# Attention and mixer on one core: a second staging buffer, ten step durations by the trace, and other warm-up products

## The chip, the core and the metric

The kernel runs on one core of a Trainium2 chip. A core has a matrix engine (TensorE, in the profile PE, with its weight loads as PEld), a vector engine (VectorE, DVE), an activation engine (ScalarE, ACT), a general engine (GpSimd, POOL), and DMA queues, here issued from SyncE (SP). The metric is the device time of one execution in microseconds. The kernel before takes 1115.07 us, the median of three runs from 1113.44 to 1115.68.

## The reference

Attention over 8 batches of 8 heads, 576 positions and a head width of 64, with a mask by blocks of 64 positions. Its output, heads side by side, is the input of a mixer: a token mixing of rank 32, and two matrices with a ReLU between them.

```python
scores = scale * np.matmul(q, k.transpose(0, 1, 3, 2))
scores = np.where(block_i >= block_j, scores, -1000000000.0)
scores = scores - np.max(scores, axis=-1, keepdims=True)
attn = np.exp(scores)
attn = attn / (np.sum(attn, axis=-1, keepdims=True) + 1e-09)
x = np.matmul(attn, v).transpose(0, 2, 1, 3).reshape(8, 576, 512)

h = x.transpose(0, 2, 1) @ U @ V            # U 576 x 32, V 32 x 576
u = x + h.transpose(0, 2, 1)
out = u + np.maximum(u @ w_ch1, 0.0) @ w_ch2    # 512 x 2048, 2048 x 512
```

All is float32, and the kernel keeps that precision by splitting values in two: a rounded part and the rest.

## The kernel before, in words

**Attention.** The 64 heads go one after the other (the loop over `h`). `split_qk` loads the transposed q and k of a head (64 x 1152), copies each to a rounded form (casts to `qa` and `kk`, L1161 on ACT or L1162 on DVE) and subtracts that from the loaded values to get the rest (`qb` and `kk`, L1168 on POOL or DVE). A DMA then puts copies of `qa` and `kk` into further partitions. `maxima` makes scores (L1256, L1254 for the first product of a head) and their row maxima (L1263), turned by L1275 (ACT) or L1276 (DVE); `probabilities` makes the scores again (L1300, L1301), their exponentials (L1322), a cast (L1325) and its rest (L1330); `apply_v` multiplies by v (L1354 to L1356) and divides (reciprocal L1364). After every second head `mix` applies U and V (L1384 to L1427; L1404 and L1406 are two of its ACT casts, L1405 a subtraction on POOL, L1413 and L1416 its last products) and stores u in DRAM.

**The mixer's two parts.** The hidden 2048 units are split. The first 768 go through `ffn_chunk` in 16 chunks of 288 tokens, two per batch: load u, scale it (L600 POOL), round it (L605 ACT, `uh`), take the rest (L606 POOL, `ul`), 72 products with w1 (L617, with L622 and L625 for the ReLU and its split) and 72 with w2 (L641). Chunks 14 and 15 belong to the last batch. Their products stand at a low priority (1e6 and up) and are what PE does between the heads' products. The other 1280 units are done by `block_products` (L906) after all attention has ended: 3360 products of 288 columns, in a scheme that multiplies sums of blocks.

**Staging of the block part's weights.** `blocks_of(n)` prepares the weights for that part while the heads run, w1 for n = 0 (from the priority of head 25) and w2 for n = 1 (from that of head 45). In six passes for n = 0 and five for n = 1 it takes a staging buffer `sg`, writes seven blocks into it, each as a rounded part (L730, ACT) and a rest (L731, POOL or DVE), makes four sums of blocks on the way (L735, POOL or DVE), and stores the whole buffer to DRAM (`w_d`, L750, on SP's queue). There is one such buffer, so a pass can write only when the store of the pass before has landed. The block part loads from `w_d` later.

**What sets the order.** All work is given as steps to `Plan.add`, each with an engine, a duration in ns, a priority, what it reads and writes, and for some steps other engines with their own durations (`others`). `Plan.issue` then runs a simulation with these numbers when the program is built, and writes each engine's instructions in the order that comes out. On each engine it takes the ready step of the smallest priority number. A step that may go to several engines is left aside on one when another would finish it sooner: `max(now, until) + duration + late` there against `now + ns + late` here, where `late` is a fixed handicap of a way. `after` is the time from a step's end until its result may be used, for DMAs the flight time (`DL` = 3000 ns). Steps on POOL and those on DVE marked shared (`port`) are not run at the same time, and such a DVE step holds POOL for 200 ns more. Durations are varied by up to 2% by a fixed rule on the step's number. Until 260 us of simulated time (`WARM`) PE gets a pair of products of zeros (L1495) whenever it has nothing ready. Steps of a head have priorities of 1000 per head: those of `split_qk` 900 ahead of their head. On the chip, each engine goes through its list in that order, and waits by semaphores for what the instruction needs.

**Start.** Before the steps stand some products of zeros (L1043), nine of 128 x 128 in float32, on a memset tile `zero` (L1032).

## Time and profile before

| | before |
|---|---|
| runs (3) | 1115.07 us median, 1113.44 to 1115.68 |
| profiled execution, its own time | 1114.15 us |
| its span | 1112.4 us |
| PE busy | 1078.8 us (97%), 10484 products |
| DVE busy | 988.1 us (89%) |
| ACT busy | 695.6 us (63%) |
| POOL busy | 382.8 us (34%) |
| first and last head's reciprocal (L1364) | 22.7 and 639.0 us |
| last mixing ends | 646.7 us |
| the run of block products (L906) on the chain of waits | 699.06 us to 1109.2 us |

The page has the busy time and the number of instructions of each engine, then the span in 40 slices, the DMA queues, the chain of work that ended last (followed back from the last instruction to what released each step), and groups of instructions by line with their mean duration and the idle time ahead of them. PE's busy time holds overlapping instructions and modelled ends, so a busy PE isn't PE at its peak. The views of the trace used below are the chain in order of time, the instructions of one line or tile, the stretches (busy time and, in brackets, the number of instructions of each engine between two times, then granted clock, DMA share and GB/s), and the listing by time, whose rows read: start, duration, engine, line, operation, what it writes and reads, and in square brackets what ended the idle time before it.

### The profile page before, as it was taken

The page shows a single profiled execution, that of the slowest core. Times are in us where ns is not written, and L with a number is a line of the kernel's source. Part 1 is how long each engine was busy: PE and PEld are TensorE (multiplying, and loading weights), DVE is VectorE, ACT ScalarE, POOL GpSimd, SP SyncE. Part 2 cuts the span into 40 slices and gives each one's busy share as a digit, 9 for nine tenths or more (in the row PEclk, how much of TensorE's full clock was granted, in tenths as well). Part 3 has the DMA queues.
Part 4 walks back from the last instruction along what each step waited for, and adds up shares of the span by engine and source line. Part 5 has one row for each costly group of instructions (what it writes and reads, how often), then busy time and mean ns, then how long its engine had stood idle before and what let it go on. Part 6 is the DMA issues. An engine that isn't in the chain of part 4 may idle for free.

```text
span 1112.4 us, 27442 instructions
## 1 busy us (share of the span) xinstructions
PE 1078.8 (97%) x10484; PEld 898.6 (81%) x10484; DVE 988.1 (89%) x2045; ACT 695.6 (63%) x1422; POOL 382.8 (34%) x494
## 2 busy tenths in 40 slices
PE   9899899999999899999999999999999999999998
PEld 8788788888888777888887777777777777777776
DVE  8899899999999889999998634798989999898987
ACT  5559876777786878768877622455555545454553
POOL 4426544657546768456387621000000000000000
PEclk9999999999999999999999999999999999999999
DMA  8763556466555565665544376312314040403111
GB/s 193 176 190 106 137 156 175 124 161 167 154 166 142 148 189 168 179 169 152 144 133 144 115 229 249 107 55 75 93 37 129 1 128 1 129 21 108 39 49 43
DMA packets 91651, 141.36 MB, mean 127 GB/s; under 512 B 14784, under 2 KB 65920, under 8 KB 91520
## 3 DMA queue, kind: packets, MB, share of 16 engines
q1 hardware_dynamic: 91520, 139.61, 43.6%
q8 instruction: 82, 1.34, 0.5%
q14 instruction: 49, 0.40, 0.1%
HBM read 83.05 MB, written 37.49 MB: 108 GB/s over the span
## 4 chain that ended last, share of the span: by engine, by line
PE 59%; DVE 22%; ACT 6%; DMA 5%; POOL 4%; issue 3%; SPq 0%; POOLq 0%; DVEq 0%; ACTq 0%
PE bb L906 37%; PE bf L641 5%; DVE pp L1330 4%; PE bf L617 4%; DVE mx L1263 4%; DMA w_d<-sg 2%; DVE hl L625 1%; PE bg L641 1%; DVE kk L1168 1%; DMA raw<-in_qk_dram 1%; ACT pp L1325 1%; PE ba L1300 1%; DVE x L1369 1%; PE ba L1256 1%; POOL wr L735 1%
## 5 line engine op out<-in xcount | busy, mean ns | idle before, releaser
L906 PEld LDWEIGHTS <-wb 128*128 128x128 f16 x3360 | 328.8, 98 | 82.8
L906 PE MATMUL bb<-hh,wb 128*128 128x288 f16 x2240 | 370.4, 286 | 0.0
L906 PE MATMUL bb<-hl,wb 128*128 128x288 f16 x1120 | 237.8, 286 | 0.0
L641 PE MATMUL bf<-hh,w2h 128*128 128x288 f16 x342 | 98.6, 288 | 0.6 <-DVE hl L625 0.5
L835 ACT CAST hh<-hb 128x576 f16<-128x576 f32 (+1 forms) x96 | 56.7, 591 | 66.6 <-PE bb L906 65.3
L641 PE MATMUL bf<-hl,w2h 128*128 128x288 f16 x342 | 97.8, 286 | 0.0
L641 PE MATMUL bf<-hh,w2l 128*128 128x288 f16 x342 | 97.8, 286 | 0.0
L641 PEld LDWEIGHTS <-w2h 128*128 128x128 f16 x768 | 75.3, 98 | 20.9 <-issue 1.5
L861 DVE TENSOR_TENSOR wr<-bb,wr 128x576 f32<-128x576 f32 (+1 forms) x120 | 77.8, 654 | 15.9 <-PE bb L906 15.9
L617 PEld LDWEIGHTS <-w1h 128*128 128x128 f16 x768 | 71.9, 98 | 22.2 <-issue 4.5
L1354 PE MATMUL ba<-vv,pp 128*128 128x65 f16 x840 | 87.7, 193 | 1.1 <-DVE pp L1330 0.9
L1356 PE MATMUL ba<-vv,pp 128*128 128x65 f16 x840 | 86.9, 191 | 1.4 <-DVE pp L1330 1.4
L1355 PE MATMUL ba<-vv,pp 128*128 128x64 f16 x840 | 87.4, 195 | 0.0
L1263 DVE TENSOR_REDUCE mx<-ba 128x1 f32<-128x192 f32 (+1 forms) x190 | 86.3, 479 | 0.8 <-PE ba L1256 0.6
L1168 POOL TENSOR_TENSOR qb<-raw,qa 64x576 fp32r<-64x576 f32 x44 | 62.5, 1421 | 56.9 <-ACT qa L1161 24.7
L1354 PEld LDWEIGHTS <-pp 128*128 128x128 f16 x840 | 77.4, 96 | 3.3 <-ACT pp L1325 0.7
L1355 PEld LDWEIGHTS <-pp 128*128 128x128 f16 x840 | 77.9, 97 | 2.5 <-issue 1.4
L1356 PEld LDWEIGHTS <-pp 128*128 128x128 f16 x840 | 78.0, 99 | 1.8 <-DVE pp L1330 1.6
L1330 DVE TENSOR_TENSOR pp<-ba,pp 128x448 f16<-128x448 f32 (+1 forms) x110 | 69.4, 644 | 2.7 <-ACT pp L1325 2.5
L617 PE MATMUL bf<-uh,w1l 128*128 128x288 f16 x368 | 69.2, 287 | 0.0
L835 ACT CAST hh<-wr 128x576 f16<-128x576 f32 (+1 forms) x72 | 42.6, 592 | 39.9 <-PE bb L906 39.9
L1300 PE MATMUL ba<-qa,kk 128*128 128x192 f32 (+1 forms) x187 | 64.9, 354 | 0.8 <-ACT ut L1427 0.5
(226 smaller groups left out, 2850.2 us busy)
## 6 DMA issues: line engine op xcount, KB each, us to landing
raw<-in_qk_dram SPq DMA_DIRECT2D x63, 288.0 KB
qb<-qa SPq DMA_DIRECT2D x64, 144.0 KB
kk<-kk SPq DMA_DIRECT2D x64, 144.0 KB
o_d<-ot SPq DMA_DIRECT2D x64, 144.0 KB
wr<-o_d SPq DMA_DIRECT2D x32, 288.0 KB
vr<-in_v_dram SPq DMA_DIRECT2D x28, 320.0 KB
wb<-w_d SPq DMA_DIRECT2D x14, 640.0 KB
out_dram<-wr SPq DMA_DIRECT2D x31, 288.0 KB
```

The costliest lines, as they stand in the source:

```text
L617: nc.tensor.matmul(ps[:, :T], w()[wn][:, k, fs], m[k].ap, start=(i == 0), stop=(i == len(ops) - 1))
L641: nc.tensor.matmul(ps[:, :T], w()[wn][:, f, ms], hs[f][x].ap, start=(i == 0), stop=(i == len(ops) - 1))
L835: add("ACT", _act(size(x), True), E, lambda: nc.scalar.copy(h(), x[0]()), [x[1]], [hb])
L861: add("DVE", _dve(size(out)), E, lambda: getattr(nc.vector, op)(out[0](), x[0](), y[0]()), [x[1], y[1]], [out[1]])
L906: nc.tensor.matmul(bank[:, i, :T], w(x, k), p.ap[:, k, :], start=first and n == 0, stop=last and n == len(ops) - 1)
L1168: sub = lambda e, dst=dst, x=x, y=y: lambda: e.tensor_sub(dst, raw[:, x], f32(y))
L1263: lambda i=i, view=view: nc.vector.tensor_reduce(out=mx[:, 96 + i : 97 + i], in_=view(), op=ALU.max, axis=AX.XY if i == 4 else AX.X, negat ...
L1300: nc.tensor.matmul(o, kk[:, 0, ks], qa[:, 64 + q0 : 64 + q1], start=True, stop=False)
L1330: lambda at=at, view=view, shaped=shaped: nc.vector.tensor_sub(shaped(pl[:, at]), view(), shaped(ph[:, at])),
L1354: nc.tensor.matmul(bank[:, o : o + D + 1], ph[:, w], vv[:, y, 0 : D + 1], start=(j == 0), stop=False)
L1355: nc.tensor.matmul(bank[:, o : o + D], ph[:, w], vv[:, y, D + 1 : 2 * D + 1], start=False, stop=False)
L1356: nc.tensor.matmul(bank[:, o : o + D + 1], pl[:, w], vv[:, y, 0 : D + 1], start=False, stop=(j == i))
```

## The change

Four things. (1) `stage_r` has two staging buffers in place of one. (2) Numbers that `Plan` works with: the flight time of the store of `w_d` goes from 3000 to 6500 ns; ten kinds of ACT steps get durations longer by 20 to 130 ns; L731 and L735 on POOL go from 60 to 130 ns of fixed time; and two DVE ways do: that of the casts L1162 from 64 to 130 ns, that of the splits L1168 from 68 to 250 ns. With 1.042 x 576 that last way counts 850 ns, and 600 of lateness stand on top, against 1340 on POOL. (3) At the start four of the float32 products of zeros stay. (4) Behind them come 32 float16 products of zeros with 256 columns, in alternating rows: eight pairs that use rows 0 to 63 for the one bank and 64 to 127 for the other, then eight pairs with rows 0 to 95 and 96 to 127. What is computed of the outputs is the same. From L1046 on, lines of the changed kernel are five higher.

```diff
@@ -412 +412 @@
-        add("ACT", _act(n, True), prio, lambda: nc.scalar.activation(f32(z), f32(upp), AF.Abs), [st], [zt])
+        add("ACT", _act(n, True) + 110, prio, lambda: nc.scalar.activation(f32(z), f32(upp), AF.Abs), [st], [zt])
@@ -605 +605 @@
-                add("ACT", _act(T, True), E, lambda us=us, h=uh: nc.scalar.copy(h.ap, us.ap), [us], [uh])
+                add("ACT", _act(T, True) + 30, E, lambda us=us, h=uh: nc.scalar.copy(h.ap, us.ap), [us], [uh])
@@ -622 +622 @@
-            add("ACT", _act(T), E, lambda ps=ps, th=th: nc.scalar.activation(th.ap, ps[:, :T], AF.Relu), [ps], [th])
+            add("ACT", _act(T) + 35, E, lambda ps=ps, th=th: nc.scalar.activation(th.ap, ps[:, :T], AF.Relu), [ps], [th])
@@ -666 +666 @@
-    stage_r = ring(ap, 1, [P, 7, 2, 2, P], F16, "sg")
+    stage_r = ring(ap, 2, [P, 7, 2, 2, P], F16, "sg")
@@ -730 +730 @@
-                add("ACT", _act(m, True), pr, lambda: nc.scalar.copy(hi, src), [b[1]], [sg.parts[k]])
+                add("ACT", _act(m, True) + 60, pr, lambda: nc.scalar.copy(hi, src), [b[1]], [sg.parts[k]])
@@ -732 +732 @@
-                add("POOL", 60 + 1.98 * m, pr, sub(nc.gpsimd), [b[1]], [sg.parts[k]], others=[("DVE", _dve(m), sub(nc.vector), True, 400)])
+                add("POOL", 130 + 1.98 * m, pr, sub(nc.gpsimd), [b[1]], [sg.parts[k]], others=[("DVE", _dve(m), sub(nc.vector), True, 400)])
@@ -736 +736 @@
-                add("POOL", 60 + 1.98 * m, pr, f(nc.gpsimd), [x[1], y[1]], [out[1]], others=[("DVE", _dve(m), f(nc.vector), True, 400)])
+                add("POOL", 130 + 1.98 * m, pr, f(nc.gpsimd), [x[1], y[1]], [out[1]], others=[("DVE", _dve(m), f(nc.vector), True, 400)])
@@ -751 +751 @@
-                [parts_d[n][q]], after=DL,
+                [parts_d[n][q]], after=6500,
@@ -973 +973 @@
-                            "ACT", _act(m * T, True), E, lambda a=at_x: nc.scalar.activation(a(), a(), AF.Relu), [x], [x]
+                            "ACT", _act(m * T, True) + 130, E, lambda a=at_x: nc.scalar.activation(a(), a(), AF.Relu), [x], [x]
@@ -1042 +1042 @@
-    for _ in range(9):
+    for _ in range(4):
@@ -1043,0 +1044,5 @@
+    halves = zero.ap.bitcast(F16)
+    for x in (64, 96):
+        for _ in range(8):
+            for bank, r in ((0, slice(0, x)), (1, slice(x, P))):
+                nc.tensor.matmul(banks_f[bank][:, 0 : 2 * P], halves[r, 0:P], halves[r], start=True, stop=True)
@@ -1162 +1167 @@
-                others=[("DVE", 64 + 0.55 * S, lambda dst=dst, x=x: nc.vector.tensor_copy(dst, raw[:, x]), True, 200)],
+                others=[("DVE", 130 + 0.55 * S, lambda dst=dst, x=x: nc.vector.tensor_copy(dst, raw[:, x]), True, 200)],
@@ -1170 +1175 @@
-                "POOL", 1340, pr, sub(nc.gpsimd), [raw, a], [b], others=[("DVE", 68 + 1.042 * S, sub(nc.vector), True, 600)],
+                "POOL", 1340, pr, sub(nc.gpsimd), [raw, a], [b], others=[("DVE", 250 + 1.042 * S, sub(nc.vector), True, 600)],
@@ -1221 +1226 @@
-                ("ACT", _act(10 * D, True) + 100, lambda: nc.scalar.activation(raw.ap, raw.ap, AF.Copy, scale=sv[:, 0:1]), False, 100),
+                ("ACT", _act(10 * D, True) + 200, lambda: nc.scalar.activation(raw.ap, raw.ap, AF.Copy, scale=sv[:, 0:1]), False, 100),
@@ -1225 +1230 @@
-            "ACT", _act(10 * D, True), pr, lambda: nc.scalar.copy(vv[:, :, 0:D], raw.ap), [raw], [vv],
+            "ACT", _act(10 * D, True) + 80, pr, lambda: nc.scalar.copy(vv[:, :, 0:D], raw.ap), [raw], [vv],
@@ -1275 +1280 @@
-            "ACT", _act(P), pr + 2, lambda: nc.scalar.activation(mr[rows], bank[rows, 0:P], AF.Copy, bias=LIFT * LN2 / SCALE), [bank], [mr],
+            "ACT", _act(P) + 130, pr + 2, lambda: nc.scalar.activation(mr[rows], bank[rows, 0:P], AF.Copy, bias=LIFT * LN2 / SCALE), [bank], [mr],
@@ -1404 +1409 @@
-        add("ACT", _act(P, True), pr, lambda: nc.scalar.copy(t3[0:R, :], tz.ap), [tz], [t3])
+        add("ACT", _act(P, True) + 55, pr, lambda: nc.scalar.copy(t3[0:R, :], tz.ap), [tz], [t3])
@@ -1427 +1432 @@
-                add("ACT", _act(n), pr, lambda bank=bank, a=a, n=n: nc.scalar.copy(ut[:, a : a + n], bank[:, :n]), [bank], [to[g]])
+                add("ACT", _act(n) + 20, pr, lambda bank=bank, a=a, n=n: nc.scalar.copy(ut[:, a : a + n], bank[:, :n]), [bank], [to[g]])
```

Three places of the order follow; rows are as they stand on the engine, one below the other, with the line, the operation, what it writes and reads, and the shape.

On POOL, before, at the end of staging (`sg` is the staging buffer, `wr` the weights that are staged, `us`, `uh` and `ul` a chunk's input of the first mixer part, `xh` and `t` belong to mixing):

```order
L731 TENSOR_TENSOR sg_132<-wr,sg_132 128x2x128
L735 TENSOR_TENSOR wr<-wr 128x256
L731 TENSOR_TENSOR sg_132<-wr,sg_132 128x2x128
L606 TENSOR_TENSOR ul_127<-us_121,uh_123 128x288
L606 TENSOR_TENSOR ul_128<-us_122,uh_124 128x288
L600 TENSOR_SCALAR us_121<-ur_120,sc 128x288
L600 TENSOR_SCALAR us_122<-ur_120,sc 128x288
L731 TENSOR_TENSOR sg_132<-wr,sg_132 128x2x128
L606 TENSOR_TENSOR ul_129<-us_121,uh_125 128x288
L606 TENSOR_TENSOR ul_130<-us_122,uh_126 128x288
L1390 TENSOR_TENSOR xh_183<-x_182,xh_183 64x128
L1405 TENSOR_TENSOR t_0_185<-tz_186,t_0_185 32x128
```

The same place in the changed program (L1173 is the old L1168, the rests of q and k; L1395 and L1410 are the old L1390 and L1405):

```order
L735 TENSOR_TENSOR wr<-wr 128x256
L606 TENSOR_TENSOR ul_129<-us_121,uh_125 128x288
L606 TENSOR_TENSOR ul_130<-us_122,uh_126 128x288
L731 TENSOR_TENSOR sg_132<-wr,sg_132 128x2x128 x3
L1173 TENSOR_TENSOR kk_186<-raw_181,kk_186 64x576
L1173 TENSOR_TENSOR qb_190<-raw_180,qa_184 64x576
L1173 TENSOR_TENSOR kk_187<-raw_180,kk_187 64x576
L1173 TENSOR_TENSOR qb_188<-raw_181,qa_182 64x576
L1173 TENSOR_TENSOR kk_185<-raw_181,kk_185 64x576
L1395 TENSOR_TENSOR xh_211<-x_209,xh_211 64x128
```

Before, no split of q or k stood on POOL between the last staged rest and mixing; now five of them do, those of the last heads.

On PE, before, around the scale of the last batch (L475, which closes its mixing; `bf` are banks of the first mixer part):

```order
L617 MATMUL bf_90<-uh_123,w1l 128x288
L617 LDWEIGHTS w1l
L617 MATMUL bf_90<-uh_124,w1l 128x288
L475 MATMUL ba_94<-rowu_118,factor_0_136 128x2
L617 LDWEIGHTS w1l
L617 MATMUL bf_90<-uh_125,w1l 128x288
L617 LDWEIGHTS w1l
L617 MATMUL bf_90<-uh_126,w1l 128x288
```

The same place in the changed program, from the last mixing products (L1418, L1421) on; the L617 rows are the first of chunk 14:

```order
L641 MATMUL bf_90<-hl,w2h 128x288
L1418 MATMUL ba_95<-ident,x_210 128x128 x3
L1421 MATMUL ba_95<-v_218,t_0_213 128x384
L1418 MATMUL ba_97<-ident,x_210 128x128 x2
L1421 MATMUL ba_97<-v_218,t_0_213 128x192
L455 MATMUL ba_94<-ident,oneu_114 1x128
L475 MATMUL ba_96<-rowu_118,factor_0_137 128x2
L617 LDWEIGHTS w1h
L617 MATMUL bf_89<-uh_123,w1h 128x288
L617 LDWEIGHTS w1h
L617 MATMUL bf_89<-uh_124,w1h 128x288
```

Before, products of chunk 13 stood on both sides of the scale; now all chunks but the last two are finished ahead of it, and the next products behind it are those that read the input scaled by it.

On PE, the first rows of the changed program (`bf` are the two banks, L1048 the new products; before, nine products of L1043 stood here, and L1495 right behind them):

```order
L1537 UNCONDITIONAL_BRANCH
L1043 MATMUL bf_89<-zero 128x128 x4
L1048 LDWEIGHTS zero
L1048 MATMUL bf_89<-zero 128x256
L1048 LDWEIGHTS zero
L1048 MATMUL bf_90<-zero 128x256
```

Five products are gone, and each of the 32 new ones has a weight load of its own.

## The prediction, made before the changed kernel was run

> **What bounds the kernel now.** I read the page first, then its chain of waits, then the stretches of the trace in which the block part's weights are staged.
>
> ```profile
> span 1112.4 us, 27442 instructions
> PE 1078.8 (97%) x10484; PEld 898.6 (81%) x10484; DVE 988.1 (89%) x2045; ACT 695.6 (63%) x1422; POOL 382.8 (34%) x494
> PE 59%; DVE 22%; ACT 6%; DMA 5%; POOL 4%; issue 3%; SPq 0%; POOLq 0%; DVEq 0%; ACTq 0%
> 699.06 410.14 PE bb L906 x3348
> ```
>
> From 699.06 us to the end the chain is nothing but block products (L906), back to back: 410.14 / 3348 = 0.1225 us each, and 3.2 us of tail. The change touches none of them. What can move is when that run starts, so all DVE time on the chain (22% of 1112.4, 245 us) lies before it: about 245 / 651 = 0.38 of the attention stage. PE is fed there by the first mixer part (L617, L641), which the order fits between heads. One head takes 9.8 us: 616.3 us between the first and the last of 64 reciprocals.
>
> ```profile
> L1364 DVE RECIPROCAL rv<-rv x64: 190/191/193, 22.7 to 639.0; 128x5 f32<-128x5 f32 x64
> 200.00:240.00 40.00, 39.83 (x449) 34.80 (x447) 38.81 (x93) 27.99 (x66) 22.31 (x23) 1.00 0.57 152
> 360.00:400.00 40.00, 36.17 (x427) 30.58 (x423) 34.64 (x77) 32.51 (x80) 28.48 (x44) 1.00 0.62 174
> 400.00:440.00 40.00, 36.66 (x404) 30.45 (x405) 37.40 (x96) 29.15 (x70) 30.65 (x45) 1.00 0.55 159
> 560.00:600.00 40.00, 36.22 (x399) 30.45 (x399) 33.51 (x86) 31.83 (x73) 33.04 (x45) 1.00 0.48 137
> ```
>
> The columns are PE, PEld, DVE, ACT and POOL busy. At 200 PE and DVE are both full. In the staging stretches neither is (PE loses 3.3 to 3.8 us in 40), while POOL does most work. So staging is where time is lost, and the two ends of it are on POOL:
>
> ```profile
> 332.46 0.68 POOL L731 TENSOR_TENSOR sg<-wr,sg 128x256 f16<-128x256 f32 x1
> 440.36 1.21 POOL L731 TENSOR_TENSOR sg<-wr,sg 128x128 f16<-128x128 f32 x3
> 555.31 1.93 POOL L731 TENSOR_TENSOR sg<-wr,sg 128x256 f16<-128x256 f32 x3 [1.23 <-ACT sg L730]
> 633.63 0.68 POOL L731 TENSOR_TENSOR sg<-wr,sg 128x256 f16<-128x256 f32 x1
> 332.46:441.57 109.11, 101.19 (x1151) 84.94 (x1150) 98.43 (x230) 81.27 (x194) 80.44 (x120) 1.00 0.56 160
> 555.31:634.31 79.00, 73.26 (x838) 61.93 (x837) 63.27 (x151) 58.44 (x139) 63.74 (x90) 1.00 0.42 123
>   DMA w_d<-sg: 10.9, 9
> ```
>
> The first stretch lasts 109.1 us for 80.4 us of POOL work (POOL waits 36% on top), the second 79.0 for 63.7 (24%). The last row, from the view of the line L730 alone, tells what ended ACT's idle time ahead of that cast: with the single buffer nine casts waited for the store to leave it, 10.9 us in all, and ACT's queue behind them.
>
> **The change, part by part.** *The splits of q and k (L1168) all go to POOL.* With a DVE price of 850 and 600 of lateness against POOL's 1340, DVE can never be the sooner way, so the order puts 128 on POOL and none on DVE; before it was 76 and 52.
>
> ```profile
> L1168 POOL TENSOR_TENSOR qb<-raw,qa 64x576 fp32r<-64x576 f32 x44 | 62.5, 1421 | 56.9 <-ACT qa L1161 24.7 <-DVE rowu L461 9.0 <-DVE kk L1162 6.7
> L1168 POOL TENSOR_TENSOR kk<-raw,kk 64x576 fp32r<-64x576 f32 x32 | 45.1, 1410 | 7.7 <-PE ba L1356 2.1 <-DVE z L396 1.5 <-DVE pp L1330 1.4
> L1168 DVE TENSOR_TENSOR kk<-raw,kk 64x576 fp32r<-64x576 f32 x32 | 29.6, 926 | 1.1
> L1168 DVE TENSOR_TENSOR qb<-raw,qa 64x576 fp32r<-64x576 f32 x20 | 15.8, 788 | 0.1
> 0.00:332.40 332.40, 22.34 (x27) 65.31 (x46) 0.99 0.59 159
> 332.40:441.60 109.20, 10.41 (x12) 10.00 (x9) 1.00 0.56 160
> 441.60:555.30 113.70, 7.26 (x8) 25.30 (x18) 1.00 0.59 163
> ```
>
> DVE loses 29.6 + 15.8 = 45.4 us and POOL gains 52 x 1.415 = 73.6 us. The last three rows, of the stretches of the trace, count L1168 alone (DVE, then POOL) before, in and after the first staging stretch: outside it 22.3 + 7.3 = 29.6 us of DVE work goes. The gain is between nothing (PE full, as at 200) and 29.6; by DVE's share of the chain 29.6 x 0.38 = 11.1. DVE also gets steps that were elsewhere (seven more casts of q or k, eleven more L1276), so I take **-8 us**.
>
> *First staging stretch.* With two buffers the store throttles staging no more, and its steps, due earlier than the next head's L1168, go first on POOL.
>
> ```profile
> L731 POOL TENSOR_TENSOR sg<-wr,sg 128x256 f16<-128x256 f32 x63 | 41.5, 673 | 19.5 <-ACT sg L730 8.5 <-DVE kk L1168 7.0 <-DVE x L1369 3.0
> L735 POOL TENSOR_TENSOR wr<-wr 128x256 f32<-128x256 f32 x36 | 26.3, 731 | 7.1 <-DVE qb L1168 2.2 <-DVE rv L1361 1.5 <-DVE qa L1162 1.5
> ```
>
> In the new order POOL's steps from the first to the last staged split (42 L731, 24 L735, 13 L1168, 30 others) come to 80.1 us at the page's mean durations, and they hold L1168 for 6.5 heads; before, 12 on DVE and 10.00 / 1.41 = 7 whole ones on POOL, 19 or 9.5 heads, fell into that stretch. POOL waits on top: between none and the 36% seen. The store's wait goes, those for ACT's casts and DVE stay, so I take half, 18%: 94.5 us. The 3 heads that are left need 29.4, together 123.9 against 109.1, +14.8. PE works on meanwhile: 66 more mixer products stand ahead of head 48 than before, 66 x 0.1225 = 8.1. Net **+6.7** (no waits: -7.7; 36%: +21.1).
>
> *Second stretch and the end of attention.* The order puts 62.1 us of POOL work from the first to the last staged split, at half of 24% on top **69.5** (62.1 to 77.0), and behind it five L1168 in a row, 7.1 us: the last heads' splits wait until all staging is done. Then the last head runs alone: copy of kk, three groups of exponentials and casts, and the way from its reciprocal to the end of mixing.
>
> ```profile
> 20.91 2.43 DMA kk<-kk
> L1322 ACT ACTIVATE bw<-bw 128x640 f32<-128x640 f32 x56 | 39.0, 696 | 9.6 <-PE bw L1301 9.3
> L1325 ACT CAST pp<-bw 128x640 f16<-128x640 f32 x56 | 39.2, 700 | 0.4
> 618.64 1.26 DVE L1168 TENSOR_TENSOR kk<-raw,kk 64x576 fp32r<-64x576 f32 x1
> 646.37 0.33 PE L1416 MATMUL ba<-v,t 96*128 96x192 f32 x1
> ```
>
> That is at least 2.4 + 3 x 1.4 + (646.7 - 639.0) = 14.3, and at most the 26.8 us that it took before (619.9 to 646.7, with staging still in ACT's queue). I take 16, near the lower end, so 7.1 + 16 = **23** after the last staged split.
>
> *What is late next.* Before, 120 products of chunk 13 covered the way from mixing to the next chunk's input. In the new order all chunks but the last two are finished there, and the next PE step after the scale (L475) is chunk 14's first.
>
> ```profile
> 655.16 0.91 ACT L605 CAST uh<-us 128x288 f16<-128x288 f32 x2 [1.28 <-POOL us L600]
> 690.24 8.82 PE bf L641 x72
> ```
>
> The input was ready at 656.07, 9.4 us after mixing ended at 646.70. Nothing covers that now: **9.4** on PE. After it come 288 mixer products and 18 block products, 306 x 0.1225 = 37.5, then 3342 x 0.1225 + 3.2 = 412.6. In return those 120 products (408 were left before, 288 now) are done earlier.
>
> *Start.*
>
> ```profile
> 1.04 4.21 PE L1043 MATMUL bf<-zero 128*128 128x128 f32 x18 [1.04 <-DVE zero L1032]
> 5.05 2.14 PE L1495 MATMUL bf<-zero 128*128 128x256 f16 x10
> 6.94 0.50 PE L1254 MATMUL bw<-kk,qa 96*128 96x288 f32 x2
> 7.83 2.36 PE L1495 MATMUL bf<-zero 128*128 128x256 f16 x20
> 5.09 0.57 DVE L1095 CAST kk<-marks 64x640 fp32r<-64x640 f32 x1
> L1495 PEld LDWEIGHTS <-zero x238: 95/98/156, 4.8 to 190.6; 128*128 128x128 f16 x119
> ```
>
> The first head's inputs stood at 5.66, but PE was in products of zeros until 6.94. Ten of them started in 1.9 us (slow clock, 0.2 each), the later twenty 0.11 apart. In place of ten passes of 0.234 (five of nine products) come 32 products on part of the rows, of which no row exists: if two run at once they cost 16 x 0.2, if not, 32 x 0.2, less what the faster clock saves after about 7 us. That puts the first real product at 7.6 to 9.4, +0.7 to +2.5; I take **+1.5**. The Trainium skill (TensorEngine Tiling (Array Packing), Key Properties) says that tiles on different rows work in parallel but that changing the tiling mode drains the engine; by the first half of that the term is +0.7, by the second nearer +2.5. Fillers grow from 238 to 280, 42 x 0.11 = 4.6 if none falls into a wait, nothing if all do: **+2**.
>
> **Sum**, against the profiled span: the first staged split of the second stretch comes at 555.3 + 1.5 + 2 - 8 + 6.7 = 557.5; + 69.5 + 23 = 650.0 is the end of mixing (646.7 before); + 9.4 + 37.5 + 412.6 = 1109.5, against 1112.4. That execution took 1114.15 in all and the median of the runs is 1115.07, 2.7 above the span: **1112**, a gain of 0.3%, the 120 products done early less the wait that they covered and POOL's delay.
>
> **Rivals.** *Faster: POOL flows.* With the store's wait gone POOL waits only 5%: the stretches cost 84.1 and 65.2, 10.4 + 4.3 us less: 1097. For it: ACT's 10.9 us for the store held up the very casts that POOL waited for. Against: 7.0 us of L731's waits were for DVE.
>
> *Slower: POOL's queue decides.* If POOL still waits 24% in both stretches, they cost 99.3 and 77.0, +4.8 and +7.5: 1124. It decides once POOL's waits pass about a fifth. For it: that is what the calmer stretch shows today, and the heads' splits can no longer go to DVE. Against: part of those 24% was the buffer. Should the *change not do what it says*, casts still waiting for a store, the 36% stay in the first stretch too: 1134.
>
> *Slower: the port.*
>
> ```profile
> L1162 DVE CAST kk<-raw x23: 426/443/1306, 62.0 to 597.4; 64x576 fp32r<-64x576 f32 x23
> ```
>
> A cast of k on DVE takes 426 ns at best and 1306 at worst, so something holds some of them. If the 51 casts of q and k that stay on DVE each met a POOL step (POOL would be busy 455 of 650 us, 0.70) and waited half of 1.42 us, DVE would carry 51 x 0.70 x 0.71 = 25.4 us, x 0.38 = 9.6, some 8 of it new: 1120. Against it: the median is 443, hardly above the minimum. The Trainium skill (SBUF — State Buffer, Who interferes with whom) has such a mechanism, a port pair that DVE's casts share with GpSimd and that whoever starts first holds for the whole instruction; the 1306 in that row agrees.
>
> **Chances.** My case (1106 to 1118): 0.43. POOL flows: 0.24. POOL's queue, the store's wait included: 0.25. The port: 0.08. A measurement of this kernel tells apart about 0.2%, 2.2 us; of my case half lies below 1112.8, 0.16 within, 0.05 above 1117.3. Faster 0.24 + 0.22 = 0.46, same 0.16, slower 0.05 + 0.25 + 0.08 = 0.38. The range leaves a tenth out at either end: 1097 to 1129.
>
> **What the new profile would show.** The step on the splits: no L1168 on DVE, POOL near 455 us busy. The staging steps: a first stretch of some 95 us and hardly a wait of L730 for w_d; a second of about 70. The end: an idle PE of 9 us ahead of the first L617 of chunk 14, with POOL or ACT as releaser. The start: the first L1254 at 7.6 to 9.4. I am wrong if heads pass at less than 9.3 us outside staging (then DVE set the pace), or if POOL waits much more or less than the 18% and 12%.

## The result, and the profile after

The changed kernel takes **1126.07 us** (median of four runs, 1123.84 to 1128.93), the kernel before 1115.38 beside it: a ratio of **1.0093**, 95% interval 1.0070 to 1.0117. It is slower by 10.7 us, where I had forecast a gain of 3; the range up to 1129 held the time, the sign was wrong.

The head of the page of the changed kernel, and two rows of its groups:

```profile
span 1123.8 us, 27528 instructions
PE 1089.2 (97%) x10548; PEld 905.4 (81%) x10548; DVE 966.9 (86%) x2016; ACT 681.3 (61%) x1401; POOL 456.9 (41%) x544
L1173 POOL TENSOR_TENSOR qb<-raw,qa 64x576 fp32r<-64x576 f32 x64 | 90.3, 1411 | 64.6 <-PE ba L1276 9.2
L1173 POOL TENSOR_TENSOR kk<-raw,kk 64x576 fp32r<-64x576 f32 x64 | 90.9, 1420 | 12.1 <-DVE z L396 5.0
```

POOL took the 74 us of splits that the order gave it, and DVE lost 21 us of work. All the same the last head's reciprocal came at 657.88 us, 18.9 us later than before.

To see where the time went I set the two traces side by side at the reciprocal of each head. Because PE may be further on in products of the first mixer part (mixer products from here on) at the same head, the difference is corrected: *behind* = start of the reciprocal minus that in the kernel before, minus 0.1225 us for each mixer product that the order has ahead of the head's last product more than before.

| behind, us, at head | 5 | 13 | 31 | 43 | 53 | 63 |
|---|---|---|---|---|---|---|
| changed kernel | 9.0 | 14.0 | 13.0 | 6.9 | 6.4 | 2.0 |

So some 14 us are lost by head 13, before any staging, though the figure swings from head to head (0.6 at head 8, 8.4 at head 12); between heads 31 and 43, where the first staging stretch lies, 6 come back, and 4 between heads 53 and 63. From +2.0 at the last head it comes to +11.4 at the end. There, 138 mixer products more than before had been done early, and PE ran dry: it had no product whose input was ready. The staged splits on POOL, from the listing by time of the changed kernel (first and last of either stretch), then the chain:

```profile
325.47 0.67 POOL L731 TENSOR_TENSOR sg<-wr,sg 128x256 f16<-128x256 f32 x1
412.13 0.43 POOL L731 TENSOR_TENSOR sg<-wr,sg 128x128 f16<-128x128 f32 x1
562.40 2.57 POOL L731 TENSOR_TENSOR sg<-wr,sg 128x256 f16<-128x256 f32 x4
627.18 1.94 POOL L731 TENSOR_TENSOR sg<-wr,sg 128x256 f16<-128x256 f32 x3
663.80 0.33 PE L1421 MATMUL ba<-v,t 96*128 96x192 f32 x1
711.18 409.41 PE bb L906 x3342
```

The stretches shrank to 87.1 and 66.7 us (109.1 and 79.0 before). In the two rows that follow (from and to, length, POOL busy) POOL's own work in them is 78.2 and 60.5 us:

```profile
325.47:412.56 87.09, 78.22 (x109) 1.00 0.59 170
562.40:629.12 66.72, 60.45 (x86) 1.00 0.50 150
```

From the last staged split to the end of mixing it took 664.13 - 629.12 = 35.0 us, and from there to the run of block products 47.05.

Why 35.0: the listing by time of SP, DVE, POOL and PE in that stretch.

```profile
630.61 1.16 SPq L1158 DMA_DIRECT2D raw<-in_qk_dram  x1
636.17 0.45 DVE L1167 CAST qa<-raw 64x576 fp32r<-64x576 f32 x1 [5.32 <-DMA raw<-in_qk_dram]
636.70 1.41 POOL L1173 TENSOR_TENSOR qb<-raw,qa 64x576 fp32r<-64x576 f32 x1 [3.16 <-DVE qa L1167]
646.96 0.75 SPq L1286 DMA_DIRECT2D qa<-mr  x1
649.92 0.34 PE L1305 MATMUL bw<-qa,kk 128*128 128x320 f32 x1
657.88 0.19 DVE L1369 RECIPROCAL rv<-rv 128x5 f32<-128x5 f32 x1
```

The load of the last head's q and k was issued at 630.61 (587.81 before). It goes into one of two buffers, which comes free when the splits that read it are done, and these stood on POOL behind all staging: the first of the five ended at 630.59. DVE, then POOL, waited for that load; the last head's splits ended at 639.59, 10.5 us after staging, and its mixing 24.5 us later. Those 24.5 us are three parts: 10.3 to the first product of the second scores (649.92), in which the head's keys are copied, its first scores and row maxima are made and the maxima are copied into `qa` (L1286); 8.0 to its reciprocal; 6.3 to the end of mixing.

And behind mixing, in stretches of 3 us on PE (busy, instructions, granted clock, DMA share, GB/s):

```profile
664.00:667.00 3.00, 0.76 (x6) 1.00 0.39 144
667.00:670.00 3.00, 0.93 (x4) 0.65 0.71 198
670.00:673.00 3.00, 1.69 (x7) 0.50 1.04 340
673.00:676.00 3.00, 3.00 (x20) 0.71 1.05 393
```

PE waits for chunk 14's input until 668.78, 4.7 us after mixing, and its clock falls to half. The Trainium skill (TensorE: Matmul & The Clock Gate, Part 1: The HAM clock gate) has this: an idle window of some 3.4 us halves the clock until a busy one has passed. The rows agree; my prediction had no term for it.

### The profile page after: what moved, and what is told of

It reads as the page before. It is cut to its first block, busy times and chain, and to the rows that moved or that the text cites. A ratio compares the mean times of both kernels' runs of the same rounds, so it can differ in the third digit from the quotient of the medians.

```text
span 1123.8 us, 27528 instructions
## 1 busy us (share of the span) xinstructions
PE 1089.2 (97%) x10548; PEld 905.4 (81%) x10548; DVE 966.9 (86%) x2016; ACT 681.3 (61%) x1401; POOL 456.9 (41%) x544
## 5 line engine op out<-in xcount | busy, mean ns | idle before, releaser
L1173 POOL TENSOR_TENSOR qb<-raw,qa 64x576 fp32r<-64x576 f32 x64 | 90.3, 1411 | 64.6 <-PE ba L1276 9.2
L641 PE MATMUL bf<-hh,w2h 128*128 128x288 f16 x372 | 107.0, 288 | 0.4 <-DVE hl L625 0.3
L641 PE MATMUL bf<-hl,w2h 128*128 128x288 f16 x372 | 106.4, 286 | 0.0
L641 PE MATMUL bf<-hh,w2l 128*128 128x288 f16 x372 | 106.4, 286 | 0.0
L1173 POOL TENSOR_TENSOR kk<-raw,kk 64x576 fp32r<-64x576 f32 x64 | 90.9, 1420 | 12.1 <-DVE z L396 5.0
L617 PEld LDWEIGHTS <-w1h 128*128 128x128 f16 x768 | 72.0, 98 | 25.7 <-issue 7.7
L1268 DVE TENSOR_REDUCE mx<-ba 128x1 f32<-128x448 f32 (+1 forms) x189 | 85.0, 477 | 1.2 <-PE ba L1261 0.8
L1335 DVE TENSOR_TENSOR pp<-ba,pp 128x448 f16<-128x448 f32 x110 | 69.6, 645 | 1.0 <-ACT pp L1330 0.7
L617 PE MATMUL bf<-uh,w1l 128*128 128x288 f16 x368 | 69.6, 290 | 0.0
L617 PE MATMUL bf<-uh,w1h 128*128 128x288 f16 x368 | 62.0, 290 | 5.2 <-ACT uh L605 3.2
```

Source lines behind the costliest of these rows:

```text
L617: nc.tensor.matmul(ps[:, :T], w()[wn][:, k, fs], m[k].ap, start=(i == 0), stop=(i == len(ops) - 1))
L641: nc.tensor.matmul(ps[:, :T], w()[wn][:, f, ms], hs[f][x].ap, start=(i == 0), stop=(i == len(ops) - 1))
L1173: sub = lambda e, dst=dst, x=x, y=y: lambda: e.tensor_sub(dst, raw[:, x], f32(y))
L1268: lambda i=i, view=view: nc.vector.tensor_reduce(out=mx[:, 96 + i : 97 + i], in_=view(), op=ALU.max, axis=AX.XY if i == 4 else AX.X, negat ...
L1335: lambda at=at, view=view, shaped=shaped: nc.vector.tensor_sub(shaped(pl[:, at]), view(), shaped(ph[:, at])),
```

## The experiments

Ratios are to runs of the kernel before on the same chip, with 95% intervals; 0.1% is 1.1 us. A profiled execution can stand some 0.5% off the median of its kernel, so the verdicts go by ratios and the traces show places. The table at the end of this section has the lag of those on which the account rests.

**The start, in the changed kernel** (its warm-up undone):

```diff
-    for _ in range(4):
+    for _ in range(9):
         nc.tensor.matmul(banks_f[0][:, 0:P], zero.ap, zero.ap, start=True, stop=True)
-    halves = zero.ap.bitcast(F16)
-    for x in (64, 96):
...
```

> The changed kernel with the nine old products of zeros at the start and none of the 32 new ones; every other instruction stands in the same order. Theory START: in the traces the first real product came 3.1 us later (10.07 against 6.94 us) and the granted clock fell to 0.91 and 0.74 between 5 and 15 us; of the 11.4 us between the spans this part is worth 3 to 4.5 us, so 1121.5 to 1123 against 1126.1. Theory SPLITS (the rest of the loss is the splits of q and k all on POOL): the same 3 to 4.5 us and no more. Rival, the start is swallowed: at head 8 the two kernels were level again (101.2 and 101.8 us), so nothing of it reaches the end: 1125 to 1127.

Measured 1.0102 (1.0082 to 1.0122): no gain. The 3 us of the start are swallowed here.

**The price of the splits alone, in the kernel before:**

```diff
-others=[("DVE", 68 + 1.042 * S, sub(nc.vector), True, 600)]
+others=[("DVE", 250 + 1.042 * S, sub(nc.vector), True, 600)]
```

> The kernel before with one number changed: the DVE way of the splits of q and k counts 250 instead of 68 ns of fixed time, so that all 128 stand on POOL. Theory SPLITS: this alone makes the early loss. In the traces the changed kernel was behind by 8 to 10 us at heads 11 to 16 once the mixer products done by then are counted (72 fewer ahead of head 12), some 3 of it from the start; the order of this kernel has the same late mixer products (60 ahead of head 12 against 108) and the same 280 pairs' worth of products of zeros (238 before). So 6 to 10 us slower than before: 1121 to 1126. Rival, my step of minus 8 for DVE holds and the loss is elsewhere: 1107 to 1115. Rival POOL QUEUE (staging with all splits on POOL and one buffer): slower by 10 or more, 1126 and up, with a longer first staging stretch than 109 us.

Measured 1.0025 (1.0007 to 1.0043): a loss, though smaller than either theory of a loss had it. With one buffer the order kept 450 mixer products for after the last head, and PE did not run dry. The outputs of this kernel are wrong (relative error 0.30) and the cause isn't known, so its time is a hint and nothing below rests on it.

**Two buffers alone:**

```diff
-    stage_r = ring(ap, 1, [P, 7, 2, 2, P], F16, "sg")
+    stage_r = ring(ap, 2, [P, 7, 2, 2, P], F16, "sg")
...
-                [parts_d[n][q]], after=DL,
+                [parts_d[n][q]], after=6500,
```

> The kernel before with two staging buffers and 6500 ns for the store of the staged weights, nothing else. Theory SPLITS: the buffers gain, as the gap between the traces shrank by 5 to 8 us in the first staging stretch and by 3 to 5 in the second: 1104 to 1112, and the waits of the casts L730 for the store (10.9 us in 9) are all but gone. Rival POOL QUEUE (the heads' splits get stuck behind staging that no longer waits): 1116 to 1124.

Measured **0.9944** (0.9925 to 0.9964). What ended ACT's idle time ahead of L730, in this kernel, holds no store any more:

```profile
  POOL wr L735: 20.2, 28
```

**Both undone, price and warm-up**, in the changed kernel (the first diff of this section, and the second reversed):

> The changed kernel with the old price for the splits (68 ns, so that DVE takes 47 of them) and the old products of zeros: what is left of the change is the two buffers and the other durations. Theory SPLITS with START: faster than before, 1104 to 1113. Rival ORDER LOTTERY (any new set of durations deals a new order, and the order before was a lucky one): 1116 to 1126, as for the whole change. Rival POOL QUEUE: 1118 to 1124.

Measured **0.9926** (0.9906 to 0.9946). Against the first experiment only the price differs: 1.0102 / 0.9926, **1.8% or some 20 us** for the step that I had put at -8. The next two split it by heads (the part of the line that changes):

```diff
-250 + 1.042 * S
+(250 if h >= 14 else 68) + 1.042 * S      # and, in the other, h < 14
```

> The changed kernel with the old price for the splits of heads 0 to 13 (68 ns, DVE may take them) and the new one (250 ns, all on POOL) from head 14 on. Measured so far, against the kernel before: all splits on POOL 1.009 to 1.010, the old price for all 0.993, so the price is worth 18 to 20 us with two buffers. Theory EARLY AND END: about half is lost by head 13, where the changed kernel was 10 to 14 us behind and the one with the old price level, the other half behind the last head, where PE waited for the last batch. Then this kernel is level at head 13 and loses the end: 1.000 to 1.004, 1115 to 1120. Rival EARLY ONLY (the end wait comes from the early loss): 0.993 to 0.997. Rival END ONLY: 1.007 to 1.011.

> The counterpart: the new price for the splits of heads 0 to 13, the old one from head 14 on. Theory EARLY AND END: 8 to 14 us behind at head 13, and no wait of some 8 us ahead of chunk 14: 1.000 to 1.005. Rival EARLY ONLY: 1.007 to 1.011. Rival END ONLY: 0.993 to 0.997.

Measured 1.0003 (0.9987 to 1.0019) and 1.0021 (0.9999 to 1.0043): against 1.0093 for the whole, taking either half away gives back 8 to 10 us. By the traces the halves aren't cleanly apart: from the last head to the end these two still lose 3.8 and 5.5 us, where the changed kernel loses 9.4.

**Staging three heads earlier** (`WQ` 45000 to 42000):

> The changed kernel with the second staging (n = 1) due three heads earlier (42000 in place of 45000), so that the last heads' splits do not stand behind it on POOL. In the trace of the changed kernel the load of q and k for the last head was issued at 630.61 us, after the last staged split (627.18 to 629.12) and two of the five splits behind it had freed its buffer, and landed 5.3 us after DVE was free for it; mixing ended at 664.1. Theory LAST LOAD: with staging out of the way the last head no longer waits, mixing ends 5 to 10 us earlier, but PE has few mixer products left and is bound by this chain, so the time falls with it: 1.000 to 1.005. Rival: DVE and PE are as full in the stretch three heads earlier, the stall only moves: 1.007 to 1.012.

Measured 1.0088 (1.0062 to 1.0115): nothing. The stall moved to head 58, PE filled it with mixer products (174 more than before by then), and the same dry stretch followed the last mixing.

**The new warm-up alone, in the kernel before:**

> The kernel before with the new products of zeros at the start (4 and 32 in alternating rows), nothing else; every other instruction stands in the same order. Theory START: the first real product 3 us later and a granted clock below 1 between 5 and 15 us, and 2 to 4 us of it reach the end, since nothing in the order gives them back: 1.002 to 1.004. Rival, swallowed: the heads of the first 100 us wait for loads of weights in any case, so 0.999 to 1.001.

Measured 1.0028 (1.0012 to 1.0045), 3.1 us, as the theory had it. The listing by time of PE:

```profile
3.06 7.06 PE L1048 MATMUL bf<-zero 64*128 64x256 f16 x32
10.05 2.31 PE L1500 MATMUL bf<-zero 128*128 128x256 f16 x10
12.02 0.83 PE L1259 MATMUL bw<-kk,qa 96*128 96x288 f32 x2
```

The first real product comes at 12.02 in this execution, 5.1 us later than before (10.07 in the changed kernel's trace). The 32 products take 7.06 us, and the ten full ones behind them (12.02 - 10.05) / 10 = 0.20 each, the slow pace. What the 32 do is in the last section.

**Fillers halved**, and **the wait at the end filled** with products of zeros, both in the changed kernel:

```diff
-        for _ in range(2):
+        for _ in range(1):
```

```diff
-now < self.warm and spare
+(now < self.warm or 649e3 < now < 662e3) and spare
```

> The changed kernel in which every filler is one product of zeros in place of a pair: 140 instead of 280, every other instruction in the same order. Theory FILLERS COST: the order has 42 more than before, and the lag at heads 11 to 31 (9 to 14 us) goes with their number; each is work that PE does ahead of real products. Without 140 of them up to 140 x 0.11 = 15 us less lag, of which 5 to 10 reach the end: 1.000 to 1.005. Rival FILLERS IN WAITS: they stand where PE would wait anyway (the first heads wait for VectorE, POOL and loads), and taking them away changes nothing, or PE's clock falls more often: 1.008 to 1.014.

> The changed kernel with 50 more pairs of products of zeros in the stretch between the last head's work and chunk 14's first product, where PE waited and its granted clock fell to 0.65, 0.50 and 0.71 for three times 3 us (9 us at a mean of 0.62, 3.4 us of full-speed work). Theory CLOCK: PE's clock stays at 1.00 there and 2.5 to 4 us come back: 1.0055 to 1.008. Rival: the wait itself is the loss and the slow products lie inside other waits: 1.009 to 1.011; the products of zeros outlast the wait: over 1.011.

Fillers halved: 1.0096 (1.0063 to 1.0129), so to some 0.3% they stand in waits and cost nothing. The wait filled: 1.0115 (1.0086 to 1.0144), not better. After the last mixing of that kernel the clock stays whole:

```profile
668.00:671.00 3.00, 3.00 (x28) 1.00 0.25 98
671.00:674.00 3.00, 3.00 (x28) 1.00 0.36 98
674.00:677.00 3.00, 3.00 (x30) 1.00 0.00 0
677.39 0.65 PE L617 MATMUL bf<-uh,w1h 128*128 128x288 f16 x4
```

But chunk 14 begins 9.4 us after mixing, behind the zeros (4.7 in the changed kernel, at half clock). What the clock gives, the zeros seem to take.

**The durations alone**, in the kernel before (one buffer, old price of the splits, old warm-up):

> The kernel before with the new durations alone (ten on ACT, the two of staging on POOL, the casts' way on DVE), one staging buffer, the old price of the splits and the old products of zeros. Two buffers alone gave 0.994, two buffers with these durations 0.993. Theory DURATIONS ARE NOTHING: 0.998 to 1.002. Rival DURATIONS GAIN, and what the buffers gained is counted twice: 0.992 to 0.996. Rival ORDER LOTTERY: any other order of this kernel than the one before is worse, 1.004 to 1.010.

Measured **0.9919** (0.9887 to 0.9950), wide but clear: the durations gain by themselves, and with the buffers it is no more (0.9926). The same with half the fillers and two buffers:

> The version with two buffers, the new durations, the old price of the splits and the old products of zeros (0.993 when run above), with one product of zeros in place of each pair of the fillers. Theory FILLERS COST: 137 x 0.11 = 15 us less of them, 3 to 8 us at the end: 0.985 to 0.990. Rival FILLERS IN WAITS: 0.992 to 0.997.

Measured 0.9943 (0.9918 to 0.9967): no gain again, as the rival had it.

**The last six heads alone at the old price**, in the changed kernel (its order is untouched up to head 56):

```diff
-250 + 1.042 * S
+(250 if h < 58 else 68) + 1.042 * S
```

> The changed kernel with the old price of the splits for heads 58 to 63 alone; up to head 56 its order is that of the changed kernel, and at head 64 it holds 1854 mixer products in place of 1980 (before: 1842). Theory END: the last heads' splits queued behind the second staging are what lets PE run dry; with DVE taking nine of them the last mixing ends some 10 us earlier, PE has cover at the scale, and 7 to 10 us come back: 1.000 to 1.003. Rival EARLY: the end wait only shows the lag that was there since head 13, and nothing comes back: 1.007 to 1.011.

Measured **1.0009** (0.9991 to 1.0027): some 9 us come back from nine splits given to DVE. Load of the last head, end of mixing, and PE behind it:

```profile
599.34 0.51 SPq L1158 DMA_DIRECT2D raw<-in_qk_dram  x1
651.77 0.34 PE L1421 MATMUL ba<-v,t 96*128 96x192 f32 x1
652.00:655.00 3.00, 3.00 (x26) 1.00 0.25 98
655.00:658.00 3.00, 3.00 (x25) 1.00 0.78 219
```

The load is issued 31 us earlier, mixing ends 12 us earlier, PE has work at full clock. So the half at the end is shown to be the price of the last heads' splits. It isn't the second staging by itself: with that three heads earlier the last head's splits began over 30 us after its end (634.66 and 601.98), and the loss stayed. In both, the heads that wait for POOL's splits let PE do its mixer products early (1980 ahead of the last head's end, 1986 with staging earlier, 1854 here), and then nothing covers the way from mixing to chunk 14.

**Another deal of the order.** `VARIANT` seeds the fixed variation of the durations by up to 2%; another number gives another order out of the same prices.

```diff
-VARIANT = 12
+VARIANT = 13      # and 11
```

> The changed kernel with another number for the fixed variation of the durations (VARIANT 13 in place of 12), which deals another order out of the same prices: here 132 mixer products stand ahead of head 12 (changed kernel 36, before 108) and 1950 ahead of head 64 (1980, 1842). Theory LOTTERY for the early half: the price does not make the early half, this one deal does, so this kernel is level with the one before at head 13, loses only the end and takes 1.000 to 1.005. Rival PRICE: all splits on POOL lose the early half in any order: 1.007 to 1.013.

> The kernel before with VARIANT 13, to see how far the deal of the order alone moves the time. Theory LOTTERY: the kernel before was a good deal among several, so another is 0.4 to 1.2% slower: 1.004 to 1.012. Rival, orders of the same prices are worth the same: 0.998 to 1.003. The difference to the changed kernel with VARIANT 13 is then the change without the deal.

> The changed kernel with VARIANT 11: 120 mixer products ahead of head 12 and 1962 ahead of head 64. Theory LOTTERY: level at head 13, the end wait stays: 1.000 to 1.006. Rival PRICE: 1.007 to 1.013.

> The kernel before with VARIANT 11, the partner of the changed kernel with VARIANT 11 (1.0013). Theory CHANGE IS NEAR NOTHING OVER ORDERS: with VARIANT 13 the change was worth 0.9995, with VARIANT 12 1.0093; here the kernel before takes 1.000 to 1.005. Rival, the change loses in most orders: 0.990 to 0.996.

| | kernel before | changed kernel |
|---|---|---|
| VARIANT 12 | 1 | 1.0093 (1.0070 to 1.0117) |
| VARIANT 13 | 1.0073 (1.0049 to 1.0097) | 1.0068 (1.0044 to 1.0093) |
| VARIANT 11 | 1.0073 (1.0053 to 1.0092) | 1.0013 (0.9996 to 1.0029) |

The changed kernel lies between theory and rival with 13, and in LOTTERY's range with 11; the kernel before with 11 is slower than either side expected. The change is worth +0.9%, nothing, and -0.6% in three deals (the last from runs on two chips, each set against the kernel before on its own). The deal alone moves the kernel before by 0.7%.

> Two buffers, the new durations, the old price of the splits and the old products of zeros (0.993 with VARIANT 12), here with VARIANT 13, in which the kernel before takes 1.0073. Theory GAIN IS REAL: buffers and durations are worth 0.7% in any order, so 1.000 and no more than 1.003. Rival DEAL: the 0.7% was a good order, 1.005 to 1.010.

Measured **0.9915** (0.9895 to 0.9936), 1107.85 us: a larger gain than the theory had. With number 13 buffers and durations gain 1.6% (0.9915 / 1.0073), so their gain stands in both deals that were tried. The price, with the warm-up, then costs 1.0068 / 0.9915, 1.5%, in this deal: nearly what it costs with number 12. This version is faster than both kernels.

How far each is behind the kernel before, by its profiled execution, at six heads and at the end of the span, and PE busy in the 12 us that follow the start of the last mixing product:

| | head 5 | 13 | 31 | 43 | 53 | 63 | end | PE busy of 12 |
|---|---|---|---|---|---|---|---|---|
| changed kernel | 9.0 | 14.0 | 13.0 | 6.9 | 6.4 | 2.0 | 11.4 | 6.38 |
| old warm-up | 6.2 | 11.4 | 13.6 | 7.9 | 10.1 | 6.1 | 14.9 | 6.38 |
| old price and warm-up | -4.3 | 0.9 | 4.9 | 3.7 | -1.4 | -4.1 | -3.8 | 12.00 |
| new price from head 14 | -0.8 | -0.5 | 5.8 | 5.9 | -1.0 | -5.0 | -1.2 | 10.15 |
| new price up to head 13 | 10.4 | 13.6 | 12.5 | 5.4 | 1.9 | -2.8 | 2.7 | 9.24 |
| old price from head 58 | 8.4 | 12.9 | 13.3 | 9.2 | 9.3 | 3.2 | 3.8 | 12.00 |
| changed, VARIANT 13 | 3.5 | 2.6 | 14.8 | 11.1 | 5.5 | 0.7 | 9.4 | 6.83 |
| changed, VARIANT 11 | 4.4 | 2.3 | 9.9 | 7.2 | -0.6 | -5.3 | 4.3 | 6.37 |
| before, VARIANT 13 | 0.8 | 0.8 | 12.5 | 12.0 | 5.8 | 8.9 | 9.9 | 12.00 |
| before, VARIANT 11 | -4.5 | 1.3 | 9.3 | 9.9 | 10.2 | 11.1 | 11.1 | 12.00 |
| old price and warm-up, VARIANT 13 | -3.9 | -0.2 | 4.4 | 5.2 | -1.5 | -7.2 | -5.6 | 12.00 |

Three things stand in it. The dry stretch at the end is in all three deals of the changed kernel and in none of the kernel before: from the last head to the end they lose 8.7 to 9.6 us, the kernels before at most 1.0, and those with the old price throughout or from head 58 on at most 1.6. The 14 us at head 13 are in one deal alone: with numbers 13 and 11 the same price leaves 2 to 3. And the price costs ahead of the end in both deals that have a partner without it: with number 13 the changed kernel is behind that partner (the last row, which has the old warm-up too) by 2.8 us at head 13, 10.4 at head 31, 7.9 at the last head and 15.0 at the end; with number 12 the figures are 13.1, 8.1, 6.1 and 15.2. So in these two deals the price makes a loss of the same size, and the deal moves the place where it shows. Number 11 has no such partner.

## Why the prediction was wrong

My sum gave the end of mixing as 650.0; it ended at 664.13. From there on it was right: 9.4 + 37.5 = 46.9 us to the run of 3342 block products, measured 47.05. So, measured by the profiled spans, the whole miss is 14.1 us, and it falls on three terms: the first staged split of the second stretch (562.40 for 557.5, **+4.9**), that stretch (66.7 for 69.5, **-2.8**) and what follows it (35.0 for 23, **+12.0**).

- *"Then the last head runs alone ... I take 16, near the lower end."* **This step failed most.** The larger part, 8.5 us, is the last head's own way: 24.5 for 16. My list of its steps (copy of kk 2.4, exponentials and casts 4.2, reciprocal to the end of mixing 7.7) left out the first scores, the row maxima with their copy, the second scores and the products with v. The trace has 10.3, 8.0 and 6.3 for the three parts, so my lower bound of 14.3 was none; in no trace of these kernels is this way under 19.3 us. The other 3.4 us: I counted five splits in a row, 7.1 us, and took the last head's data as there. The splits free the buffer that the last head's load needs, so the load was issued at 630.61, the fourth split waited 3.2 us for it, and the row took 10.5. The last six heads' price is worth 0.84% (1.0093 to 1.0009).
- *"I take -8 us" for the splits leaving DVE.* Wrong in sign. In this deal of the order the price on the first 14 heads costs 0.9%, some 10 us (1.0093 to 1.0003). DVE's share of the chain, 0.38, was no measure of what relief on DVE is worth: DVE's busy time fell by 21 us and its idle time grew. The heads take turns on a row of engines, and a split that takes 1.41 us on POOL in place of 0.79 to 0.93 on DVE may lie on that row; this is argued, not shown. With number 13 the price costs 7.9 us by the last head too, though little by head 13. Which wait makes the loss ahead of the end is not settled.
- *First stretch +6.7.* Wrong in sign. POOL's work was estimated well (80.1 us, measured 78.2), its waits were not: 87.1 us is 11% on top and not 18%. My own sum with 87.1 gives -0.7, and the stretch gave back some 6 us. The second had 10% on top (66.7 for 60.5) and not 12%. The rival that POOL flows, with 5%, was nearer in both stretches (84.1 and 65.2) and missed the end.
- *Start +1.5, fillers +2.* The first real product came at 10.07 against 6.94, +3.1, above my bound of 2.5, and 12.02 in the kernel with the new warm-up alone. Half of the products ran two at once, as the lower bound had it; the other half, 96 and 32 rows in turn, ran one after the other and took up to 0.32 us each, more than the 0.2 of my upper bound. Alone the start is worth 0.28%; in the changed kernel it is hidden. Fillers: nothing that shows, inside the bound.
- *"Nothing covers that now: 9.4".* Right in size, though half of it is made up of products at half clock.
- *POOL's queue decides, 1124* came nearest in time, but by luck: POOL waited 11% and 10% inside the stretches and not 24%, and the loss came ahead of them and behind them.
- *The port.* The shifts L396 of the 128x384 loads show some of it (groups by line in the first 160 us; busy us, mean ns; first the kernel before, then the changed one):

```profile
L396 DVE SCALAR_TENSOR_TENSOR z<-st,z 128x384 int32<-128x384 int32 x8 | 4.4, 551 | 0.1
```

```profile
L396 DVE SCALAR_TENSOR_TENSOR z<-st,z 128x384 int32<-128x384 int32 x8 | 7.0, 869 | 0.1
```

2.6 us in eight steps. In the changed kernel four of the eight began 0.3 to 0.6 us after a POOL step and took 0.81 to 1.64 us; the four that met none took 0.55 to 0.56. What it costs at the end was not tried.

What I had not asked at all: how good the order before was among its like. Two other deals of the same kernel are 0.7% slower, so by these two a change that deals anew may start from there. The measured 0.9% is the price of the splits (1.8% with number 12), less the gain of buffers and durations (0.7% there). With number 13 the two are 1.5% and 1.6%, and the change comes to nothing.

## What to carry to other kernels

Where steps of a late stage queue behind a long stretch on an engine, follow the buffers that they free: the next load waits there, and its whole chain counts; write that chain down from the trace, step by step, before it is given a time. A helper engine's relief is worth what the waits of that stage say, not its share of the chain. And where a scheduler deals the order, run the old kernel and each part of the change in a few other deals before 1% is put down to the change.

## What the runs showed beyond that

- Products that use a part of the rows and alternate between the parts overlapped in one split and not in the other. The groups of the 32 products by shape, in the kernel with the new warm-up alone, first 10 us:

```profile
L1048 PE MATMUL bf<-zero 64*128 64x256 f16 x16 | 1.9, 414 | 0.0
L1048 PE MATMUL bf<-zero 96*128 96x256 f16 x8 | 3.1, 393 | 0.0
L1048 PE MATMUL bf<-zero 32*128 32x256 f16 x8 | 3.1, 390 | 0.0
```

  Sixteen products on halves of the rows start within 1.82 us (3.06 to 4.88), 0.11 each, the two of a pair at most 5 ns apart; a full one takes 0.21 at this pace. The sixteen on 96 and 32 rows in turn need 5.17 us, 0.32 each. In the changed kernel's trace, where PE reaches its fast pace at 5.7 us, they come down to 0.21, and full ones there are 0.11 apart. The Trainium skill (TensorEngine Tiling (Array Packing), Key Properties) lets different tiles work in parallel; the trace agrees for the halves, and for 96 and 32 rows it doesn't show it. Why these cost more than full ones was not tried.
- With the new products PE comes to its fast pace late or loses it again. The listing by time, then stretches on PE, of the changed kernel:

```profile
3.06 5.61 PE L1048 MATMUL bf<-zero 64*128 64x256 f16 x32
8.00:10.00 2.00, 2.00 (x14) 0.79 1.17 249
10.00:12.00 2.00, 2.00 (x10) 0.50 1.08 351
12.00:14.00 2.00, 2.00 (x18) 0.86 0.80 165
```

  In seven of the ten traces with the new products the granted clock falls to half for 3.4 us, from 7.5 to 9.2 us on; in the other three the clock records begin only at 13.1 to 13.8 us, and full products are at the slow pace (0.21 us) until then. In nine of the ten with the old ones (the tenth has half the fillers) the fast pace comes at 4.1 to 7.1 us and holds for 34 us or more. Whether it is the rows left out that matter or the weight load ahead of each was not tried.
- Half of the fillers could go without an effect that these runs tell apart, in two kernels (1.0093 and 1.0096; 0.9926 and 0.9943). In the profiled execution of the second the granted clock was 0.50 from 12 to 42 us, where it was 1.00 with all fillers.
